# The last sixteenth of the first half of the output weights by six GpSimd transfers instead of SyncE's load

## The chip, the core and the metric

The kernel runs on one core of a Trainium2 chip. The metric is the device time of one execution in microseconds (us), the median of several runs. A profile of one execution gives the span from its first to its last instruction and the times of the single instructions and transfers in it; such times below count from the start of that span.

A core has five engines that run their own instruction streams beside each other: PE (TensorE, matmuls), DVE (VectorE), ACT (ScalarE), POOL (GpSimd) and SP (SyncE, which here only issues transfers and waits). They wait for each other through semaphores. Loads from HBM into the on-chip memory SBUF (128 partitions) are carried by 16 DMA engines.

## What is computed

One token is decoded: attention with 32 query heads over 4 cached key and value heads of 65,536 positions, a small gated MLP, and a gate that mixes the two. In short:

```python
def _A_ref(x, k_cache, v_cache, wq, wo):          # Hq 32, Hkv 4, Sk 65536, Dh 128, D 1024
    q = (x @ wq)...                               # 32 heads of 128
    scores = einsum('bhqd,bhkd->bhqk', q, k) * Dh ** -0.5
    o = einsum('bhqk,bhkd->bhqd', softmax(scores), v)
    return o.reshape(B, Sq, Hq * Dh) @ wo         # wo: 4096 x 1024

def _B_ref(x, w_in, w_sp, b_sp, w_out):           # F 3584, one position
    z = gelu(x @ w_in)
    z1, z2 = z[..., :F // 2], layernorm(z[..., F // 2:])
    return (z1 * (z2 * w_sp + b_sp)) @ w_out

g = sigmoid((x * gate_w).sum(-1))
out = g * _A_ref(...) + (1 - g) * _B_ref(...)
```

All inputs are bf16. The caches are 128 MB, the weights `wq` and `wo` 8 MB each.

## The kernel before

**The stream of loads.** Nearly everything that the kernel reads passes once through a ring in SBUF, `RING`, with five places of 16,384 bf16 columns (32 KB in each partition). The list `stream` holds the loads in the order in which they are wanted: `wq`, then keys and the MLP's weights, then pairs of key blocks (`load_k2`) and value blocks (`load_v2`), in the end the values 12 to 15 and the output weights `wo`. `load` appends to that list; `issue` turns entries into transfers on SP's queue, each as soon as the places it will overwrite have been given up (`done`), and always in the order of the list. A load waits for semaphores, on SP, until the last readers of each 1,024-column piece of its place (`("slot", i)`) have finished.

**The output weights** come last, in five loads. `("wo", 0, 0)` is the first half of the matrix, its rows 0 to 2047: partition p holds the sixteen rows 16p to 16p+15 side by side, 32 KB in all (the function `rows`, with c = 16). It goes to the first place of the ring, whose sixteen pieces hold key block 15 before. Then follow `("wo", 2, 0)` (2 MB) and the last quarter in pieces of 5, 2 and 1 eighths (`WO_CUT`: 1,280, 512 and 256 KB).

**The work at the end**, in the order in which it is queued on PE: `pv_piece(12)` to `(15)` multiply the probabilities with the values; `out_first(3)` sums the last group's denominators (L560); `wo_rows` multiplies the attention output of the first two groups with the first half of `wo`, sixteen rows per partition in a loop over c = 0..15, two halves of 512 columns each, into the PSUM tile `scp`; `out_rest(3)` scales and rearranges the last group's output (DVE, and PE at L582); `spin` runs a few matmuls whose results nobody reads; `spread` copies `scp` to SBUF on ACT (L661) and adds it to the final accumulator `fbt` with 16 matmuls (L665); `wo_piece(2)` and three `wo_piece(3, ...)` do the other half of `wo` (L717, 64 matmuls a quarter); a DVE cast (L778) and SP's store (L365) end it.

**How dependences are made.** `Recorder.op` takes an engine, a function, the keys that it reads and those that it writes, and works out the semaphore waits: an operation waits for the last writer of what it reads, and for the last writer and the readers of what it overwrites. A transfer's semaphore rises by 16 when it has landed. Every matmul pair shares its weights through `mm` (L258 to L264): the first of two loads them, which shows as L261, the second (L263) doesn't.

POOL's own work in this kernel is 36 small instructions: constants in the first 8 us, and four copies for each group of queries (`q_piece`, L487), the last at 244 us.

Of the kernel before, what the change touches and what calls it, by code (L numbers as in the profile page):

```python
# [138 lines left out]
def bass_gated_mix__gqa_block_cached__mixer_gmlp__decode_kernel(  # L139
# [19 lines left out]
    DO = A_wo.shape[1]  # L159
# [25 lines left out]
    OFF = {}  # L185
# [17 lines left out]
    arena = nc.alloc_sbuf_tensor("arena", [128, NA], BF16)  # L203
# [7 lines left out]
    def vw(base, off, dims, p0=0, np_=128):  # L211
        ps = base.ap[0][0]
        return bass.AP(tensor=base.tensor, offset=base.offset + off + p0 * ps,
                       ap=[[ps, np_]] + [list(d) for d in dims])
# [37 lines left out]
    KSC = lambda n: ("scp", n % 2)  # L252
# [3 lines left out]
    P = R.op  # L256

    def mm(e, loaded, *a, **kw):  # L258

        if not loaded:  # L260
            return e.matmul(*a, **kw)  # L261
        with nc.discard():
            one = e.matmul(*a, **kw).ins  # L263
        return e.add_instruction(dataclasses.replace(one, name=nc.get_next_instruction_name(), ldweights=False))  # L264
# [37 lines left out]
    stream = []  # L302
# [4 lines left out]
    def load(keys, src, off):  # L307

        n = len(stream)
        w = src.shape[1]  # L310
        for i, key in enumerate(keys):
            place[key] = (n, off + i * (w // len(keys)), w // len(keys))
        stream.append((keys, off, src))

    def rows(w, i, c):

        return w[128 * c * i:128 * c * (i + 1), :].rearrange("(p c) n -> p (c n)", c=c)
# [37 lines left out]
    WO_AT = [0, 8 * DO, 16 * DO, 24 * DO]  # L355
    WO_CUT = [(0, 5), (5, 7), (7, 8)]
    load([("wo", 0, 0)], rows(A_wo, 0, 16), WO_AT[0])
    load([("wo", 2, 0)], rows(A_wo, 2, 8), WO_AT[2])
    for c0, c1 in WO_CUT:
        load([("wo", 3, c0)], rows(A_wo, 3, 8)[:, DO * c0:DO * c1], WO_AT[3] + DO * c0)  # L360
# [11 lines left out]
    def grains(off, w):  # L372
        return list(range(off // GRAN, (off + w + GRAN - 1) // GRAN))

    def issue():

        while issued[0] < len(stream):
            n = issued[0]
            keys, off, src = stream[n]
            w = src.shape[1]  # L380
            gr = grains(off, w)
            if any(k not in used for x in gr if x in owner for k in owner[x]):
                return
            for j, x in enumerate(gr):
                owner[x] = (keys[j * len(keys) // len(gr)],)
            P("SP", lambda e, o=OFF["RING"] + off, w=w, src=src: e.dma_start(arena[:, o:o + w], src),
              w=[("slot", x) for x in gr], dma="s%d" % gr[0])
            issued[0] += 1

    def use(key):  # L390
        n, off, w = place[key]
        assert n < issued[0], key
        return arena[:, OFF["RING"] + off:OFF["RING"] + off + w], [("slot", x) for x in grains(off, w)]

    def done(key):
        used.add(key)
        issue()

    issue()


# [8 lines left out]
      r=["m32"], w=["sel"])  # L410
    P("DVE", lambda e: e.tensor_reduce(mq, vw(idf, 0, [[1, 16], [16, 8]]), AXX, ALU.add), r=["idf"], w=["mq"])
    P("DVE", lambda e: e.tensor_reduce(mhalf, vw(idf, 0, [[32, 2], [64, 2], [1, 32]]), mybir.AxisListType.XY, ALU.add),
      r=["idf"], w=["mhalf"])
# [4 lines left out]
    for fe in range(4):  # L418
        P("POOL", lambda e, fe=fe: e.tensor_copy(vw(sele, 128 * fe, [[32, 4], [1, 32]]),
                                                vw(idb, 64 * (fe // 2) + fe % 2, [[0, 4], [2, 32]])),  # L420
          r=["idb"], w=[KSE])
# [5 lines left out]
    def f(e):  # L427
# [7 lines left out]
      r=["oneb", "wsp", "bsp"], w=["mb"])  # L435
# [6 lines left out]
      r=["ones", "gs"], w=[KTB])  # L442
# [4 lines left out]
      r=["g"], w=["omg"])  # L447
# [3 lines left out]
    wqs, keys = use(("wq", 0))  # L451
# [242 lines left out]
    def wo_rows():  # L694
        sl, keys = use(("wo", 0, 0))

        def f(e):
            for c in range(16):
                j = c % 4
                z = 31 + 32 * c  # L700
                for s in range(2):
                    o = DO * c + 512 * s
                    ins = mm(e, s > 0, scp[32 * j:32 * j + 1, 512 * s:512 * (s + 1)], ovz[:, z:z + 1], sl[:, o:o + 512],
                             start=(c < 4), stop=(c >= 12), tile_position=(0, 32 * j),
                             skip_group_check=True)
            return ins
        P("PE", f, r=[("ovec", 0), ("ovec", 1)] + keys, w=[KSC(0)])
        done(("wo", 0, 0))

    def wo_piece(i, c0=0, c1=8):  # L710
# [54 lines left out]
    for n in (12, 13, 14, 15):  # L765
        pv_piece(n)
        if n < 14:
            pt_half(n + 2)
    out_first(3)
    wo_rows()  # L770
    out_rest(3)
    spin(2)
# [39 lines left out]
```

## Time and profile before

| | |
|---|---|
| median of 3 runs | 380.71 us (380.64 to 380.71) |
| span of the profiled execution | 379.59 us |
| read from HBM | 162.01 MB, 427 GB/s over the span |
| busy PE / DVE / ACT / POOL | 229.6 / 204.7 / 23.3 / 8.2 us |
| share of DMA in the chain that ended last | 68% |
| value load 12 (v12) landed | 338.80 us |
| value load 14 (v14) landed | 358.11 us |
| first half of `wo` issued, landed | 329.4, 367.75 us |
| next quarter of `wo` landed | 372.61 us |
| last quarter's three pieces landed | 375.72, 376.95, 377.55 us |

The profiled execution's span and the median of the runs differ by 1.12 us; that lies outside the first and last instruction. A landing is the time of a transfer's last semaphore increment: the loads raise theirs by one for each of the 16 DMA engines, so the trace has sixteen times for each load. It also has a record of every packet that a DMA engine moved, with its queue, size, start and duration, but not with the number of the engine. Engines' busy times overlap and do not add up to the span; what matters is which wait ends last at each place.

### The profile page before, as it was taken

The page shows a single profiled execution, that of the slowest core. Times are in us where ns is not written, and L with a number is a line of the kernel's source. Part 1 is how long each engine was busy: PE and PEld are TensorE (multiplying, and loading weights), DVE is VectorE, ACT ScalarE, POOL GpSimd, SP SyncE. Part 2 cuts the span into 40 slices and gives each one's busy share as a digit, 9 for nine tenths or more (in the row PEclk, how much of TensorE's full clock was granted, in tenths as well). Part 3 has the DMA queues.
Part 4 walks back from the last instruction along what each step waited for, and adds up shares of the span by engine and source line. Part 5 has one row for each costly group of instructions (what it writes and reads, how often), then busy time and mean ns, then how long its engine had stood idle before and what let it go on. Part 6 is the DMA issues. An engine that isn't in the chain of part 4 may idle for free.

```text
span 379.6 us, 2565 instructions
## 1 busy us (share of the span) xinstructions
PE 229.6 (60%) x1444; PEld 57.4 (15%) x835; DVE 204.7 (54%) x162; ACT 23.3 (6%) x24; POOL 8.2 (2%) x36
## 2 busy tenths in 40 slices
PE   0061488458558923895389428952896199737296
PEld 0010011011111200122012001220111011211024
DVE  4011496778389524974597248745773387412021
ACT  1000000010420000002200000022000000220000
POOL 5000000000000000000000000000000000000000
PEclk9997599696859985998599859995799589958599
DMA  9999999999999999999999999999999999999996
GB/s 442 421 414 394 483 388 439 439 453 391 437 442 442 442 430 435 435 442 442 442 430 394 421 442 442 444 435 428 435 435 437 435 442 442 430 421 414 418 428 263
DMA packets 3662, 162.17 MB, mean 427 GB/s; under 512 B 452, under 2 KB 452, under 8 KB 708
## 3 DMA queue, kind: packets, MB, share of 16 engines
q1 hardware_dynamic: 3616, 162.01, 98.9%
q8 instruction: 9, 0.15, 0.1%
q10 hardware_dynamic: 36, 0.00, 0.0%
q14 instruction: 1, 0.01, 0.0%
HBM read 162.01 MB, written 0.00 MB: 427 GB/s over the span
## 4 chain that ended last, share of the span: by engine, by line
DMA 68%; PE 16%; DVE 14%; ACT 1%; issue 1%; ACTq 0%; SPq 0%
DMA arena<-in_A_k_cache_dram 47%; DVE arena L499 12%; DMA arena<-in_A_wo_dram 8%; DMA arena<-in_A_v_cache_dram 7%; PE scp L261 6%; PE scp L263 5%; DMA arena<-in_B_b_sp_dram 5%; PE obt L261 2%; PE obt L263 2%; DVE arena L536 1%; PE fbt L717 1%; ACT arena L531 1%; ACTq L288 0%; PE fbt L665 0%; ACT arena L661 0%
## 5 line engine op out<-in xcount | busy, mean ns | idle before, releaser
L499 DVE STREAM_TRANSPOSE arena<-arena 128x2048 f32<-128x2048 f32 x64 | 143.0, 2284 | 56.7 <-DMA arena<-in_A_k_cache_dram 41.8
L261 PE MATMUL scp<-arena 128*128 128x512 bf16 (+1 forms) x274 | 111.5, 423 | 95.7 <-DVE arena L499 95.4
L263 PE MATMUL scp<-arena 128*128 128x512 bf16 (+1 forms) x275 | 110.4, 418 | 0.0
L261 PE MATMUL obt<-arena 128*64 128x512 bf16 (+2 forms) x334 | 61.4, 410 | 14.2 <-DMA arena<-in_A_v_cache_dram 14.2
L263 PE MATMUL obt<-arena 128*64 128x512 bf16 (+2 forms) x334 | 61.0, 408 | 0.0
L261 PEld LDWEIGHTS scp<-arena 128*128 128x128 bf16 (+1 forms) x274 | 27.4, 104 | 206.6 <-issue 103.5
L536 DVE STREAM_TRANSPOSE arena<-arena 128x2048 bf16<-128x2048 bf16 x7 | 16.2, 2311 | 27.0 <-PE obt L263 24.8
L531 ACT ACTIVATE arena<-arena 128x2048 bf16<-128x2048 f32 x8 | 16.0, 2002 | 218.4 <-DVE arena L528 195.0
L261 PEld LDWEIGHTS obt<-arena 128*64 128x64 bf16 (+1 forms) x334 | 17.9, 111 | 65.7 <-issue 59.0
L516 DVE TENSOR_SCALAR_CACHE_REDUCE arena<-scp 128x2048 f32<-128x2048 f32 x8 | 18.3, 2291 | 16.0 <-PE scp L263 16.0
L565 DVE RECIPROCAL arena<-mbt 128x1 f32<-128x1 f32 x4 | 0.6, 139 | 17.5 <-PE mbt L560 17.5
L539 DVE STREAM_TRANSPOSE arena<-arena 128x1024 bf16<-128x1024 bf16 x2 | 2.5, 1245 | 12.9 <-PE obt L263 12.9
L487 POOL COPY arena<-arena 32x32 bf16<-32x32 bf16 x16 | 3.2, 203 | 234.4 <-PE scp L263 209.8
L434 PE MATMUL mbt<-arena 1*128 1x2 bf16 x1 | 0.2, 159 | 12.2 <-DMA arena<-in_B_b_sp_dram 12.2
L436 DVE COPY arena<-mbt 128x2 f32<-128x2 f32 x1 | 0.2, 159 | 12.2 <-PE mbt L434 12.2
L578 PE MATMUL mbt<-arena 128*64 128x128 bf16 x8 | 1.3, 313 | 7.7 <-DVE arena L572 7.7
L429 PE MATMUL scp<-arena 8*128 8x1 bf16 x8 | 0.7, 198 | 8.6 <-DVE arena L424 8.6
L717 PE MATMUL fbt<-arena 128*32 128x128 bf16 x128 | 4.1, 220 | 1.2 <-DMA arena<-in_A_wo_dram 1.2
L778 DVE CAST arena<-fbt 36x128 bf16<-36x128 f32 x1 | 0.3, 282 | 7.2 <-PE fbt L717 7.2
L528 DVE TENSOR_REDUCE arena<-mbt 128x1 f32<-128x32 f32 x4 | 0.8, 192 | 6.0 <-PE mbt L525 6.0
L717 PEld LDWEIGHTS fbt<-arena 128*32 128x32 bf16 x128 | 3.6, 97 | 2.4 <-issue 1.2
L464 DVE CAST arena<-obt 97x1024 bf16<-97x1024 f32 x1 | 1.2, 1225 | 4.8 <-PE obt L263 4.8
(92 smaller groups left out, 54.9 us busy)
## 6 DMA issues: line engine op xcount, KB each, us to landing
arena<-in_A_k_cache_dram SPq DMA_DIRECT2D x2, 4096.0 KB, 33.3
arena<-in_B_w_in_dram SPq DMA_DIRECT2D x1, 7168.0 KB, 30.5
arena<-in_A_wo_dram SPq DMA_DIRECT2D x1, 4096.0 KB, 38.3
arena<-in_B_w_out_dram SPq DMA_DIRECT2D x1, 3584.0 KB, 21.4
arena<-in_A_wo_dram SPq DMA_DIRECT2D x1, 2048.0 KB, 27.2
arena<-in_A_wo_dram SPq DMA_DIRECT2D x1, 1280.0 KB, 29.9
arena<-in_A_wo_dram SPq DMA_DIRECT2D x1, 512.0 KB, 30.7
arena<-in_A_wo_dram SPq DMA_DIRECT2D x1, 256.0 KB, 30.8
```

The lines of the kernel that those rows point to most:

```text
L261: return e.matmul(*a, **kw)
L263: one = e.matmul(*a, **kw).ins
L464: P("DVE", lambda e: e.tensor_copy(psb[0:97, :], ob[0:97, :]), w=["psb", "ob"])
L487: P("POOL", lambda e, pb=pb: e.tensor_copy(vw(qpad, 24 + 32 * pb, [[QP, 4], [1, 8]], 32 * pb, 32), vw(qall, 8 * g, [[32, 4], [1, 8]], 32 * ...
L499: P("DVE", lambda e: e.transpose(ktb(i).bitcast(F32), sl[:, 4096 * p:4096 * (p + 1)].bitcast(F32)), r=keys[4 * p:4 * p + 4], w=[("kt", i % ...
L516: P("DVE", lambda e: e.tensor_scalar(scs(j), scp[:, :], 0.0, None, op0=ALU.add, op1=ALU.max, accum_out=maxc[:, j:j + 1]), w=[("sc", j % 2) ...
L528: P("DVE", lambda e: e.tensor_reduce(gcol(g, K_NB), mb[:, 0:32], AXX, ALU.min), w=[("nb", g), "mb"])
L531: P("ACT", lambda e: e.activation(psb2, scs(j), ACTF.Exp, bias=gcol(j // 2, K_NB), scale=SCALE, accum_out=lp[:, j:j + 1]), r=[("sc", j % 2 ...
L536: P("DVE", lambda e: e.transpose(ptsb2, psb2), r=["psb"], w=[("ptsb", 0), ("ptsb", 1)])
L539: P("DVE", lambda e: e.transpose(ptsb(n), ab("PSB", 1024, 1024 * (n % 2))), r=["psb"], w=[("ptsb", n % 2)])
L578: ins = e.matmul(mb[64 * g:64 * (g + 1), 0:128], vw(sel, 128 * c, [[2, 64]]), osc[:, 128 * c:128 * (c + 1)], start=(c == 0), stop=(c == 3) ...
L717: ins = e.matmul(fb[32 * b:32 * (b + 1), 0:QW], ovz[:, z:z + 32], sl[:, o:o + QW], start=False, stop=(i == 3 and c == 7), tile_position=(0 ...
```

## The change

SP's load of the first half of `wo` is cut by one sixteenth: it brings 15 of each partition's 16 rows. The sixteenth row of each (c = 15; 2 KB in a partition, 256 KB in all) is loaded by POOL in six transfers that take 16, 51, 4, 34, 6 and 17 partitions, one after the other on POOL's queue. The first waits for the readers of the sixteenth piece of the ring's place; the others wait for nothing of their own and follow it. Each row is fetched as two pieces of 512 columns, in swapped order, so that the first 512 columns of the place hold the second half of the row; `wo_rows` reads them accordingly for c = 15. All six raise one semaphore, and `wo_rows` waits for them too. Each is issued with `single_packet=True`.

```diff
     load([("wo", 0, 0)], rows(A_wo, 0, 16), WO_AT[0])
+    SPLIT = (len(stream) - 1, 15)
+    SHARES = (16, 51, 4, 34, 6, 17)
+    assert sum(SHARES) == 128
     load([("wo", 2, 0)], rows(A_wo, 2, 8), WO_AT[2])
...
                 owner[x] = (keys[j * len(keys) // len(gr)],)
+            if n == SPLIT[0]:
+                w = DO * SPLIT[1]
+                spread_rows(OFF["RING"] + off + w, src[:, w:], ("slot", gr[SPLIT[1]]))
+                src, gr = src[:, :w], gr[:SPLIT[1]]
             P("SP", lambda e, o=OFF["RING"] + off, w=w, src=src: e.dma_start(arena[:, o:o + w], src),
               w=[("slot", x) for x in gr], dma="s%d" % gr[0])
             issued[0] += 1
+
+    def spread_rows(o, src, key):
+
+        p0 = 0
+        for i, n in enumerate(SHARES):
+            dst = vw(arena[:, o:o + 1], 0, [[512, 2], [1, 512]], p0, n)
+            s0 = src[p0:p0 + n, :]
+            s0 = bass.AP(tensor=s0.tensor, offset=s0.offset + 512, ap=[list(s0.ap[0]), [-512, 2], [1, 512]])
+            P("POOL", lambda e, dst=dst, s0=s0: e.dma_start(dst, s0, single_packet=True),
+              w=[key] if i == 0 else [("share", i)], dma="sw")
+            p0 += n
...
-                    o = DO * c + 512 * s
+                    o = DO * c + 512 * (s if c < SPLIT[1] else 1 - s)
...
-        P("PE", f, r=[("ovec", 0), ("ovec", 1)] + keys, w=[KSC(0)])
+        P("PE", f, r=[("ovec", 0), ("ovec", 1)] + keys + [("share", i) for i in range(1, len(SHARES))], w=[KSC(0)])
```

## The prediction

> **What bounds the kernel now.** I read the page first. Its slices say that the loads never pause, and its queue table that they are all SyncE's (q1):
>
> ```profile
> DMA  9999999999999999999999999999999999999996
> ...
> q1 hardware_dynamic: 3616, 162.01, 98.9%
> q8 instruction: 9, 0.15, 0.1%
> q10 hardware_dynamic: 36, 0.00, 0.0%
> ```
>
> The 16 DMA engines are busy from start to end, so time is bytes over rate, but for the last slice. The chain of waits in order of time, over the end, shows what comes then (start, us, what):
>
> ```profile
> 345.79 29.93 DMA arena<-in_A_wo_dram
> 375.72 0.14 issue
> 375.86 2.16 PE fbt L717 x64
> 378.01 0.02 issue
> 378.04 0.28 DVE arena L778
> ```
>
> The chain gives the whole 2.16 us to PE. The timeline adds that PE's last eight weight loads wait once more:
>
> ```profile
> 377.59 0.23 PEld L717 LDWEIGHTS fbt<-arena 128*32 128x32 bf16 x8 [0.15 <-DMA arena<-in_A_wo_dram]
> ```
>
> That is the last load, of 256 KB; 2.0 us of fixed work follow its landing (eight weight loads and matmuls, the cast, the store). So the end is set by the last engine to deliver its sixteenth of that load. The table of stretches shows how evenly the engines get there (after the stretch: its length, busy PE, PEld, DVE, ACT, POOL; the last two columns are the DMA share and GB/s):
>
> ```profile
> 375.20:375.50 0.30, 0.17 (x1) 0.00 (x0) 0.00 (x0) 0.00 (x0) 0.00 (x0) 1.00 1.04 416
> 375.50:375.90 0.40, 0.04 (x2) 0.07 (x4) 0.00 (x0) 0.00 (x0) 0.00 (x0) 1.00 0.65 261
> 375.90:376.20 0.30, 0.30 (x13) 0.30 (x15) 0.00 (x0) 0.00 (x0) 0.00 (x0) 1.00 0.59 239
> ...
> 376.40:376.70 0.30, 0.30 (x19) 0.30 (x14) 0.00 (x0) 0.00 (x0) 0.00 (x0) 1.00 0.57 219
> ...
> 376.90:377.10 0.20, 0.20 (x14) 0.19 (x10) 0.00 (x0) 0.00 (x0) 0.00 (x0) 1.00 0.22 82
> ```
>
> The share falls to about 10/16 at 375.5 and stays there for over a microsecond: six engines are out of work, ten are not. The sixteen increments of the last load's semaphore say it engine by engine: six at 375.87 to 375.95, one at 376.21, nine from 376.76 to 377.55. The cause is in the packet records: nine times before, an instruction fetch (q8, 16 KB, eight times; q14, 8 KB, once) took an engine out of its stream. The one at 329.57 lasted 0.94 us, where a 16 KB packet of q1 takes 0.61, and the 64 KB packet behind it took 2.92 us for 2.42: 1.4 us lost. Every load is cut into sixteen equal parts, so an engine once late stays late. Idle share times length from 375.5 on sums to 0.9 us; that is all that perfect levelling could give.
>
> **The change, part by part.**
>
> *Removed from SP's load.* Each of 128 rows goes from 32 KB to 30 KB. Packets of 32 KB take 1.213 us and of 16 KB 0.611, so 2 KB is 0.075; with eight rows on each engine, each sheds 0.60 us.
>
> *Added on the POOL queue.* Each row comes as two pieces of 1 KB. Packets of 2 KB take 84 ns, of 256 B 18 ns, of 4 B 9 ns; on that line 1 KB is 46 ns (38 if the fixed part is paid once for many). Six completions at 9 ns add 0.05 on each engine, if each posts on all sixteen.
>
> *Who carries them.* No trace row shows a POOL transfer. Those of 128 rows go to all engines evenly, and ACT's two loads of 8 rows are 16 packets of 256 B: one row to an engine. I take it that a transfer goes to the largest number of engines up to 16 that divides its rows: 16 rows to 16 engines, 51 to three by 17, 4 to four, 34 to two by 17, 6 to six, 17 to one. The last five fill 3+4+2+6+1 = 16 engines once if each starts where the one before stopped. So six engines get 18 rows, ten get 2: as many as the trace has early and late ones. That they are the same ones the trace can't show, as packets carry no engine number; the equal counts are why I lean to it. [...]
>
> *Sum by engine.* Light: 4 x 0.046 + 0.05 - 0.60 = **-0.36** (-0.40 at 38 ns). Heavy: 36 x 0.046 + 0.05 - 0.60 = **+1.12** (+0.81). The last landing, on a light engine, goes from 377.55 to 377.19; the heavy ones go from 375.95 to 377.07, just below.
>
> *Cost of a visit.* A POOL packet sits between two of SP's. ACT's small ones cost their own 9 to 18 ns, and the 64 KB packets behind them kept their 2.418: lower bound, nothing more. Upper bound: a fetch lost 1.4 us for data worth 0.61, 0.8 over; six visits would be 4.8. I take the lower, since ACT's, like POOL's, are data and completions for SBUF, and a fetch is not.
>
> *When they come.* POOL waits only for slot 15's reader, the last k transpose (L499), which ends at 319.56, and POOL has no other work left. SP issues the shortened load behind v14 as now, at 329.43. So the six travel inside v12's stream and push v12 and v14 back by 0.24 on the late engines (338.80 and 358.11 become 339.04 and 358.35). That moves pv_piece(12) to (15), hence out_first(3) and out_rest(3), by 0.24. wo_rows now starts at 367.80, just behind the load's landing at 367.75 (367.39 after); it would start at 368.04 behind PE's queue, be done at 369.9, and spread's matmuls would end at 372.1 instead of 371.9. The next load lands at 372.61 - 0.36 = 372.25: 0.1 of cover left. Were it gone, wo_piece(2) would slip, which spin(3) and the wait to 375.36 hide (0.5 now). SP's issue of wo 3 waits for pv_piece(12) (345.42, then 345.66) with the ring full to 372: free. GpSimd's own time for six issues is unknown, but has 48 us until wo_rows. PE's wait for the six is one more instruction.
>
> *Total.* -0.36 on the last landing; the 2.0 us behind it are the same. Span 379.59 to 379.23; with the 1.12 between span and median (380.71), **380.35 us**.
>
> **The rivals.**
>
> *No levelling* (the six are dealt out evenly, or the equal split was no loss). Each engine gets 8 rows back: 16 x 0.046 + 0.05 - 0.60 = +0.19, **380.9**. Against it: 51, 34 and 17 do not split evenly. [...]
>
> *The shares sit on the wrong engines*: the slower case that I weigh most. If the engine that is latest now carries 18 rows, it lands at 377.55 + 1.12 = 378.67: **381.83**. It decides as soon as one heavy engine is late by over 0.25 us (377.19 - 1.12 = 376.07, against 375.95 or less for the six). For it: no number of an engine in the trace, and an unknown start of the dealing. [...]
>
> *A fetch meets a heavy engine.* The trace has a tenth fetch, at 377.16, in PE's matmuls for the second-last load; it meets an engine that is already idle. With everything 0.36 earlier it comes at 376.80. If it goes to an engine not yet hit, that is one of the six, and their packets now end 376.63 to 376.78 (375.51 to 375.66 plus 1.12). On an overlap of a packet or two the engine loses up to 1.4: 377.07 + 1.42 = 378.49, **381.65**. The margin is 0.02; cheaper pieces (38 ns) widen it to 0.33.
>
> *The six land late.* ACT's one-element loads landed at 16.54 and 21.37 because each packet waited a turn of 2.42 behind SP's. If each 1 KB piece took its own turn, a heavy engine needs 42 turns, and from 319.6 SP's ring has 32 packets until 372. wo_rows would wait till about 375 instead of 367.8, with spread (1.0 + 1.1), wo_piece(2) (2.0), spin (0.8) and the last 64 matmuls (2.1) behind it: some 6 us, **386.7**. Against it: the code asks for a single packet. [...]
>
> **How the numbers follow.** Levelling as summed 0.52; no levelling 0.08; wrong engines 0.15; the fetch 0.12; late landing or dear visits 0.07; 0.06 for a gain that I have no mechanism for (a light engine cannot shed over 0.60, so it would have to come from other fetches moving). A measurement of this kernel tells about 0.2%, 0.76 us, from no change. The first two lie within it: same 0.60. The next three are slower: 0.34. Faster 0.06. The likeliest case alone spans 380.25 (-0.45, all 12 KB at full rate and visits free) to 380.7. The range, 380.2 to 381.9, adds the wrong engines and the fetch.
>
> **What would show it.** Right: a POOL queue with 262,144 bytes and landings by 350; packets that fill the stretch 375.5 to 376.6 (share near 1 where it is 0.6); the last load's sixteen increments within 0.4 us of each other, the last near 377.2; wo_rows waiting for PE's queue, not for a load. Wrong: increments still spread over 1.5 us or more (engines), a fetch between the last packets (fetch), wo_rows later than 368.5 (late landing), or SP's packets longer than 2.42 behind each POOL packet (visits).

## The result, and the profile after

The changed kernel takes **388.71 us** (median of 4 runs, 388.55 to 389.93) where the kernel before takes 380.71 beside it (380.64 to 380.94): a ratio of 1.0217 [1.0203, 1.0232], **slower by 8.0 us**. The forecast was 380.35. The profiled execution is the longest of the four: 389.93 us, with a span of 388.5, which is 8.9 more than before. Times below compare this span with the one before.

The slices and the queue table of the page after:

```profile
span 388.5 us, 2572 instructions
...
DMA  9999899999999999999999999999999999999991
...
DMA packets 4238, 162.17 MB, mean 417 GB/s; under 512 B 948, under 2 KB 948, under 8 KB 1284
...
q1 hardware_dynamic: 3616, 161.75, 97.3%
q0 software_dynamic: 576, 0.27, 0.3%
```

The queue q0 is POOL's and has moved what it should. But it did so in 576 packets, and the last slice, which was at 6 tenths, is at 1: the stream of loads no longer reaches to the end. The chain of waits over the end (start, us, what) shows what does:

```profile
371.05 0.54 PE mbt L578 x4
371.58 4.98 another core or an unknown queue
376.56 0.14 issue
376.70 0.60 PE scp L261 x4
...
380.35 1.03 ACT arena L679
...
381.42 1.07 PE fbt L683 x16
382.49 1.79 PE fbt L735 x64
...
385.03 1.92 PE fbt L735 x64
386.95 0.02 issue
386.97 0.28 DVE arena L796
```

The chain doesn't know the releaser of the second line; it ends at 376.56, when the semaphore of the six transfers is full. The timeline of the same kernel names the wait on PE's side, in the brackets:

```profile
319.25 4.84 POOL L404 DMA_DIRECT2D arena<-in_A_wo_dram  x6 [73.95 <-DVE arena L517]
...
376.70 0.60 PE L261 MATMUL scp<-arena 128*1 128x512 bf16 x4 [5.12 <-DMA arena<-in_A_wo_dram]
```

So `wo_rows` (scp) started at 376.70, before at 367.80: 8.9 us later, as much as the spans differ by. Behind it stands work that the loads used to cover: `spread` on ACT (L679) and PE (L683), `wo_piece(2)` and the last `wo_piece` (L735). The six were issued at 319.25 and took 57 us to land. The last piece of SP's stream came at 381.04 (before 377.55) and PE was not waiting for it: its 64 weight loads at L735 ran through in one group, without the second wait of before.

The stream itself also got slower. The table of stretches, after (stretch, length, busy time of PE, PEld, DVE, ACT, POOL, then PEclk, DMA share, GB/s):

```profile
319.20:329.20 10.00, 9.74 (x78) 2.94 (x41) 3.37 (x5) 2.10 (x2) 4.84 (x6) 1.00 1.03 423
329.20:339.00 9.80, 0.61 (x4) 0.34 (x4) 4.09 (x7) 2.09 (x2) 0.00 (x0) 0.67 0.99 403
339.00:350.00 11.00, 8.39 (x64) 2.04 (x32) 2.49 (x2) 0.00 (x0) 0.00 (x0) 0.83 1.06 415
350.00:360.00 10.00, 0.00 (x0) 0.00 (x0) 0.00 (x0) 0.00 (x0) 0.00 (x0) 0.65 0.88 354
360.00:370.00 10.00, 8.68 (x56) 2.45 (x30) 0.00 (x0) 0.00 (x0) 0.00 (x0) 0.67 0.98 394
...
376.70:381.00 4.30, 4.30 (x38) 0.83 (x21) 0.29 (x1) 0.65 (x1) 0.00 (x0) 0.58 0.74 301
```

The same stretches before:

```profile
329.20:339.00 9.80, 1.12 (x10) 0.74 (x9) 4.71 (x7) 2.10 (x2) 0.00 (x0) 0.60 1.00 430
339.00:350.00 11.00, 9.84 (x64) 2.19 (x30) 2.36 (x2) 0.00 (x0) 0.00 (x0) 0.74 1.00 435
350.00:360.00 10.00, 1.75 (x10) 0.58 (x6) 0.13 (x1) 0.00 (x0) 0.00 (x0) 0.58 1.00 433
360.00:370.00 10.00, 9.80 (x99) 3.02 (x51) 1.90 (x4) 0.24 (x1) 0.00 (x0) 0.91 0.94 406
```

From 329.2 to 370 the rate is lower by 27, 20, 79 and 12 GB/s; times the lengths that is 1.4 MB less, or 3.2 us at 433 GB/s. The first half of `wo` on SP's queue indeed landed 3.2 us later (370.93 for 367.75). Over half of that, 1.8 us, comes from 350 to 360 alone, where the run with the wait hidden, below, with the same six transfers, has 392 GB/s and not 354. While `wo_rows` ran, from 376.70 to 380.35, the granted clock was 0.50, and it took 3.6 us; before, it had 1.00 and took 1.9.

**How POOL's packets went.** q0's records are 32 packets of 2 KB and 48 of 4 KB with data, 64 of 8 B and 336 of 16 B without, and 96 of 4 B (the semaphore: six transfers times sixteen engines). The data are dealt as the prediction had it: the first transfer 2 KB to each of 16 engines, the 51 rows to three engines (eight packets of 4 KB and one of 2 KB each), 4 rows to four, 34 to two, 6 to six, 17 to one. But an engine that has no rows of a transfer gets as many small packets instead: all sixteen make the fullest engine's 1+9+1+9+1+9 data turns and six completions, 36 in all (576 packets over sixteen engines). From 323.38 to 376.12 each of these turns waited for one packet of SP's, and SP's packets get shorter towards the end: on average an engine moved 14.4 of 64 KB (2.60 us each), 8 of 30 KB (1.21), 8 of 16 KB (0.66), 2.3 of 10 KB (0.41) and 4 completions (0.01) in that time, 36.7 packets of SP's and 53 us in all. Two things add up: many turns, and at each a packet of SP's to wait for. The experiments take them apart.

### The profile page after: what moved, and what is told of

Read it like the earlier page. It is cut to its first block, busy times and chain, and to the rows that moved or that the text cites. A ratio compares the mean times of both kernels' runs of the same rounds, so it can differ in the third digit from the quotient of the medians.

```text
span 388.5 us, 2572 instructions
## 1 busy us (share of the span) xinstructions
PE 230.2 (59%) x1444; PEld 57.5 (15%) x835; DVE 204.5 (53%) x162; ACT 23.3 (6%) x24; POOL 13.1 (3%) x42
## 4 chain that ended last, share of the span: by engine, by line
DMA 60%; PE 21%; DVE 16%; another core or an unknown queue 1%; ACT 1%; issue 1%; ACTq 0%; SPq 0%
DMA arena<-in_A_k_cache_dram 46%; DVE arena L517 15%; DMA arena<-in_A_v_cache_dram 8%; PE scp L261 6%; PE scp L263 6%; DMA arena<-in_B_b_sp_dram 5%; PE obt L261 3%; PE obt L263 3%; PE fbt L735 1%; DVE arena L554 1%; PE fbt L683 1%; ACT arena L549 1%; ACT arena L679 1%; ACTq L288 0%
## 5 line engine op out<-in xcount | busy, mean ns | idle before, releaser
L404 POOL DMA_DIRECT2D arena<-in_A_wo_dram x6 | 4.8, 810 | 74.0 <-DVE arena L517 74.0
L609 DVE TENSOR_TENSOR arena<-mbt,arena 64x128 f32<-64x128 f32 (+1 forms) x4 | 1.2, 290 | 9.0 <-PE mbt L600 7.8
L735 PE MATMUL fbt<-arena 128*32 128x128 bf16 x128 | 3.9, 219 | 0.0
```

Source lines behind the costliest of these rows:

```text
L404: P("POOL", lambda e, dst=dst, s0=s0: e.dma_start(dst, s0, single_packet=True), w=[key] if i == 0 else [("share", i)], dma="sw")
L735: ins = e.matmul(fb[32 * b:32 * (b + 1), 0:QW], ovz[:, z:z + 32], sl[:, o:o + QW], start=False, stop=(i == 3 and c == 7), tile_position=(0 ...
```

## The experiments

"Full" is the time at which POOL's semaphore was full; "mean landing" is the mean of the last load's sixteen increments (before: 376.68, the last at 377.55), which tells what the stream lost without the spread among engines.

**One transfer of 128 rows.**

```diff
-    SHARES = (16, 51, 4, 34, 6, 17)
+    SHARES = (128,)
```

> The same 256 KB by POOL, but as one transfer of 128 rows instead of six. Turn theory (every packet of POOL's ring waits behind one packet of SP's on the same DMA engine, and all sixteen engines make the 36 turns of the six transfers, with stuffing where they have no rows): 8 rows of two pieces are 4 packets of 4 KB and a completion on each engine, 5 turns instead of 36; the semaphore is full by 323.4 + 5 x 2.7 = 337, far ahead of the load's landing near 368, and wo_rows waits for the load again; 381 to 382 us (0.19 for the dearer pieces, and up to 1 if SP's loads run 8% slower for those 12 us). Rival, POOL's transfers are late as such (GpSimd writes descriptors slowly, or the pieces of 1 KB are slow): 256 KB are 256 KB, wo_rows waits again to about 376 and it stays near 388. Rival, the unequal shares load six engines too much: fixed here, 381 as well; e2_short tells it from the first.

380.89 us (380.60 to 381.06), ratio 1.0004 [0.9995, 1.0013]. Full at 337.86, mean landing 376.49, SP's 64 KB packets 2.421 us. Five turns on each engine:

```profile
q0 software_dynamic: 80, 0.26, 0.2%
```

The same bytes by the same queue cost nothing when they come in 80 packets and not 576. What is slow is how they are dealt, and not that GpSimd carries them.

**Shorter turns.** SP's two value loads ahead of the half are cut to packets of 16 KB; as a control, the same in the kernel before.

```diff
-            P("SP", lambda e, o=OFF["RING"] + off, w=w, src=src: e.dma_start(arena[:, o:o + w], src),
+            m = 16384 if SPLIT[0] - 2 <= n < SPLIT[0] else 65536
+            P("SP", lambda e, o=OFF["RING"] + off, w=w, src=src, m=m: e.dma_start(arena[:, o:o + w], src, max_dma_last_dim=m),
```

> The six transfers as they are; only SP's loads of the values 12 and 14 come in pieces of 16 KB instead of 64 KB, so that a turn behind one of SP's packets lasts 0.66 us instead of 2.4 to 2.7. Turn theory: 36 turns x 0.66 are 24 us, the six are in by 347 to 350, wo_rows waits for the load again, and the time is 380.7 plus what the visits cost the stream: 381 to 383. Rival, lateness of POOL's transfers as such, or six overloaded engines: neither is changed by SP's piece size, the semaphore fills near 376 again and it stays near 388.5. If the visits cost SP's stream a fixed amount each (0.1 us), its last landing stays 3.5 us late; if the stream runs 8% slower only while POOL's ring holds work, it is 1.5 to 2 us late.

> The kernel before with the values 12 and 14 in pieces of 16 KB: the control for e2_short. Each piece pays some 9 ns more than its bytes (a packet of 16 KB takes 0.611 us, one of 64 KB 2.418): 48 more packets on each engine are 48 x 9 = 0.43 us. 381.1, by every theory.

The control: 381.00 (380.79 to 381.19), ratio 1.0007 [0.9997, 1.0016]; short packets alone cost little. The changed kernel with them: **383.14** (382.90 to 383.47), 1.0065 [1.0050, 1.0080]. POOL still has 576 packets, but is full at 350.01. Its chain of waits ends on SP's last load again:

```profile
347.19 30.37 DMA arena<-in_A_wo_dram
377.56 0.14 issue
377.70 1.77 PE fbt L736 x56
379.47 0.04 issue
379.51 0.42 PE fbt L736 x8
```

So the wait is the number of turns times the length of a packet of SP: POOL's packets now pass in 25 us (324.26 to 349.57), 0.70 a turn behind packets of 0.63 to 0.68 us, where the changed kernel's 64 KB packets took 2.60. The wait goes, and 5.6 of the 8.0 us with it. 2.4 us stay, and the mean landing (378.78) has 2.1 of them; the short packets themselves account for 0.3, by the control.

**The wait hidden.** The sixteenth row leaves `wo_rows` and is multiplied by eight small matmuls behind `wo_piece(2)`, straight into `fbt`.

```diff
-            for c in range(16):
+            for c in range(15):
...
+    def wo_last():
+        sl, keys = use(("wo", 0, 0))
...
+            for s, b, j in SLOTS:
+                o = DO * 15 + (QW * s + 512) % DO
+                z = 31 + 32 * 15 - j
+                ins = e.matmul(fb[32 * b:32 * (b + 1), 0:QW], ovz[:, z:z + 32],
+                               sl[:, o:o + QW], start=False, stop=False,
...
+    wo_last()
```

> The six transfers and SP's load as in the changed kernel; the row c = 15 is taken out of wo_rows and multiplied behind wo_piece(2) by eight matmuls straight into the final accumulator, so nothing but those eight waits for the six. Turn theory: the six still land near 376.5, but wo_rows starts with the load near 371, and the end is again the last landing of the last load, 381.0 in the changed kernel, plus 2.0: span 383.1, 384.2 us. That leaves +3.5 of the +8.0 as the price that SP's stream pays for the visits, and 4.5 as the wait of wo_rows with its slow clock. Rival, the whole loss is one thing, the late semaphore: 380.4 to 381.

**383.45** (383.38 to 383.51), 1.0072 [1.0057, 1.0087], although POOL is full only at 375.96. The chain of waits ends on the load:

```profile
346.44 31.79 DMA arena<-in_A_wo_dram
378.23 0.14 issue
378.36 2.13 PE fbt L748 x64
```

With the transfers as they were and only their reader moved, 5.3 of the 8.0 us go: this is the price of `wo_rows` waiting, its slow clock included. The other 2.7 are the price on SP's stream (mean landing 379.38, 2.7 later). Two experiments that change different things agree on this division within 0.3 us, or 0.6 when the 0.3 of the short packets is taken off the first.

**Without `single_packet`.**

```diff
-            P("POOL", lambda e, dst=dst, s0=s0: e.dma_start(dst, s0, single_packet=True),
+            P("POOL", lambda e, dst=dst, s0=s0: e.dma_start(dst, s0),
```

> The changed kernel without single_packet=True. The trace of the changed kernel shows POOL's data in packets of at most 4 KB (four pieces of 1 KB) with the flag set. If the flag does nothing there: 576 packets on POOL's queue, 36 turns, the six full near 376, 388 to 390 us. If it does something, packets and turns get more and it is slower than 389.

388.47 (388.13 and 388.81), 1.0205 [1.0185, 1.0226]; packets of the same number and sizes, full at 375.21. In the queue table:

```profile
q0 software_dynamic: 576, 0.27, 0.3%
```

The flag did nothing in this kernel. A packet held at most four pieces of 1 KB with it and without it. The mean landing is 378.96 here, 2.3 later than before.

**Is it the small packets?** My first theory for the stream's 2.7 us was the packets without data. Eight equal transfers have none; (96, 15, 17) has them, with the same 16 turns.

```diff
-    SHARES = (16, 51, 4, 34, 6, 17)
+    SHARES = (16,) * 8
```

> The same rows by POOL in eight transfers of 16 rows, one row to each engine in each: no engine is without rows, so there is no stuffing; 8 x (1 packet of 2 KB and 1 completion) = 16 turns, in by 323.4 + 16 x 2.43 = 362, before the load. Stuffing theory (SP's packets slow down behind the stuffing packets of 4 to 16 bytes and not behind data): SP's 64 KB packets keep their 2.42 us, last landing within 0.5 of the kernel before, 380.5 to 381.2. Rival, every visit and every additional transfer costs SP's stream 0.1 us: 16 visits, last landing +1.6, 382 to 382.5.

> The same rows by POOL in three transfers of 96, 15 and 17 rows: also 16 turns (4 + 2 + 10), but of these nine are stuffing of 16 bytes on fifteen engines, while the one with the 17 rows has data; one engine carries 24 rows. Stuffing theory: SP's 64 KB packets take 2.5 to 2.7 us while the 17 rows are under way, the mean landing of the last load is 1 to 1.5 us later than in e5_nostuff, 382 to 383 us. Rival, visits cost the same whatever they carry: the mean landing as in e5_nostuff, and the time differs from it by the loaded engine alone (16 more rows, 1.3 us on one engine). The mean over the engines, not the last one, tells the two apart.

The theory fell. Eight equal transfers, 256 packets of which none is of 16 or 8 B: 383.94 (383.31 to 384.96), 1.009 [1.007, 1.011], mean landing 379.49, full at 361.77. With stuffing, (96, 15, 17): 382.49 (382.07 to 382.89), 1.0048 [1.0033, 1.0063], mean landing 377.83, full at 360.19. The one without is the dearer one. SP's 64 KB packets took 2.70 us on average in 324 to 334 there. In the other kernel they took 2.60 while the 96 rows were under way (323.7 to 334.9), and these have no stuffing; from 340.1 on, while the 17 rows and their stuffing were, 2.46.

**The shares on SP's queue.** Whole rows of 2 KB, on the queue that carries the rest, in shares of 64, 51 and 13.

```diff
-    SHARES = (16, 51, 4, 34, 6, 17)
+    SHARES = (64, 51, 13)
...
-            P("POOL", lambda e, dst=dst, s0=s0: e.dma_start(dst, s0, single_packet=True),
+            P("SP", lambda e, dst=dst, s0=s0: e.dma_start(dst, s0),
```

> The row c = 15 on SP's own queue, in whole rows of 2 KB, by transfers of 64, 51 and 13 rows: no POOL, no turns, no stuffing. If SP's transfers are dealt by the largest divisor too, three engines get 4 + 17 + 1 = 22 rows, ten get 5 and three get 4. Tests what levelling alone would bring: if the three are early ones, the late engines shed 3 to 4 rows, 0.25 to 0.3 us, the last landing goes from 377.55 to 377.3, and 380.4 us. If one of the three is late: 14 rows more, 1.1 us, 381.8. The six landing late has no part in it by any theory.

381.86 (381.51 to 381.97), 1.0029 [1.0017, 1.0041]. There are no turns between queues here, and it is still 1.2 us slower. The expectation had 381.8 for a late engine that carries 14 rows more, but that is not what happened: the mean landing is 377.70, 1.0 later, and the last only 0.8 behind that, so that it wasn't the loaded engines alone that were late. While three engines moved the 51 rows, SP's first 30 KB packets rose to as much as 1.94 us (undisturbed they take 1.138), and the 2 KB packets took 0.09 to 0.24 for 0.084. So rows that come in such shares disturb the other packets on SP's queue too.

**Are several transfers under way the trouble?** Four transfers of 32 rows, and the same with each waiting for the one before.

```diff
-    SHARES = (16, 51, 4, 34, 6, 17)
+    SHARES = (32,) * 4
...
-              w=[key] if i == 0 else [("share", i)], dma="sw")
+              w=[key, ("share", 0)] if i == 0 else [("share", i), ("share", i - 1)], dma="sw")
```

> The stuffing theory has fallen: without stuffing, eight transfers slowed SP's packets as much. What is left goes with the number of POOL's transfers that are under way together: one alone (e1_even) left SP's 64 KB packets at 2.42 us, three cost the mean landing of the last load 1.1 us, eight 2.8. Here the rows come by four transfers of 32 (one packet of 4 KB and one completion on each engine in each: 8 turns), issued one right after the other. Theory of transfers under way together: SP's packets take 2.55 to 2.8 us for the 20 us that the turns last, mean landing 0.8 to 1.4 late, 381.4 to 382.2 us. Rival, only the number of turns counts: e1_even's 5 turns cost nothing, so 8 cost next to nothing, 380.7 to 381.0.

> As e8_four, but each transfer is issued only when the one before has landed, so that one at a time is under way; the same 8 turns, packets and bytes. Theory of transfers under way together: SP's packets stay at 2.42 us, 380.6 to 381.1, though the last of the four lands later (four times some 7 us, near 350, still before the load). Rival, turns or transfers as such: as e8_four.

Together: 382.54 (382.25 to 390.22 in seven runs), 1.0060 [1.0031, 1.0090]. One at a time: 382.51 (382.18 to 385.63 in six), 1.0069 [1.0039, 1.0099]. No difference, so this theory fell too. The traces are of executions of 386.54 and 384.85 us, longer than the medians. In the second's, 64 KB packets were slow while a transfer had its visits (means of 2.45 to 2.9 in steps of 2 us) and back at 2.42 to 2.46 between the transfers.

**Neighbouring rows, or rows apart?** The same four and eight transfers, but transfer i takes partitions i, i + 4, i + 8 and so on (i + 8 for eight): each is spread over all 128 partitions.

```diff
-    SHARES = (16, 51, 4, 34, 6, 17)
+    SHARES = (32,) * 4
...
-            dst = vw(arena[:, o:o + 1], 0, [[512, 2], [1, 512]], p0, n)
-            s0 = src[p0:p0 + n, :]
+            dst = vw(arena[:, o:o + 1], 0, [[512, 2], [1, 512]], i, n)
+            dst = bass.AP(tensor=dst.tensor, offset=dst.offset, ap=[[len(SHARES) * dst.ap[0][0], n], [512, 2], [1, 512]])
+            s0 = src[i:i + 1, :]
...
-            s0 = bass.AP(tensor=s0.tensor, offset=s0.offset + 512, ap=[list(s0.ap[0]), [-512, 2], [1, 512]])
+            s0 = bass.AP(tensor=s0.tensor, offset=s0.offset + 512, ap=[[len(SHARES) * s0.ap[0][0], n], [-512, 2], [1, 512]])
```

> e9_serial was as slow as e8_four, so the number of transfers under way together is not the reason either. What e1_even has and the others lack: each of its engines moves rows that lie 8 partitions (and 256 KB of wo) from its neighbour's; in the others the sixteen engines work on the same 16 to 51 neighbouring partitions at a time. Here four transfers of 32 rows as in e8_four, but transfer i takes the partitions i, i+4, i+8, ..., all over SBUF. Crowding theory: SP's 64 KB packets keep 2.42 us, mean landing of the last load within 0.3 of the kernel before, 380.6 to 381.1. Rival, more than one transfer as such: as e8_four, 382.3 or more.

> As e5_nostuff, eight transfers of 16 rows, but transfer i takes the partitions i, i+8, i+16, ...: the same 16 turns, packets and bytes as there, one row for each engine in its own eighth partition. Crowding theory: 380.6 to 381.2, SP's packets at 2.42. Rival, more than one transfer as such: as e5_nostuff, 383.3 to 385.

Four apart: **380.79** (380.59 to 380.89), 1.0002 [0.9993, 1.0012], mean landing 376.56, SP's 64 KB packets 2.418 to 2.421, 128 packets on q0 as with four neighbouring ones. Eight apart: 381.51 (381.27 to 381.99), 1.0019 [1.0010, 1.0029], above the 380.6 to 381.2 that was expected; mean landing 377.11, SP's 64 KB packets 2.44 to 2.48, 256 packets as with eight neighbouring ones. The first stretch in which POOL's packets run beside SP's, with eight transfers of neighbouring rows:

```profile
324.00:334.00 10.00, 6.16 (x54) 2.25 (x30) 4.45 (x7) 2.10 (x2) 0.13 (x1) 0.86 0.99 382
```

and with eight transfers of rows apart:

```profile
324.00:334.00 10.00, 5.69 (x48) 2.08 (x26) 4.69 (x8) 2.10 (x2) 0.00 (x0) 0.94 1.00 428
```

382 against 428 GB/s (421 in the same stretch before), with the same bytes, packets and turns. Which rows a transfer takes changes the price on the stream: 1.8 us to nothing for four transfers (382.54 to 380.79), 3.2 to 0.8 for eight (383.94 to 381.51).

Why it does is not shown, and being neighbours can't be all of it. The 96 rows of (96, 15, 17) cover three quarters of the partitions, six rows to an engine, and while they were under way, ahead of the other two transfers, SP's 64 KB packets took 2.60 us. With all 128 rows in one transfer they took 2.42. The stretch 324 to 334 with the 96 rows, and with the 128:

```profile
324.00:334.00 10.00, 5.64 (x50) 2.05 (x28) 4.74 (x8) 2.10 (x2) 0.00 (x0) 0.99 0.99 394
324.00:334.00 10.00, 6.16 (x56) 2.12 (x31) 4.81 (x9) 2.10 (x2) 0.00 (x0) 0.91 1.04 446
```

The rate of a stretch also depends on where packets of 64 KB begin and end (446 with the 128 rows and 421 before, at the same 2.42 us a packet), so the packets' length is the surer measure.

No trace shows which rows an engine takes; the expectation for four apart assumed that they are dealt in order. On that assumption another reading, a conjecture too, fits as well: an engine's packets are slow when its POOL rows are not among the eight that SP's loads give it. With eight apart 0.8 us stays by either. No run separates the two.

## Why the prediction was wrong

**The step that failed is *When they come*.** It let the six "travel inside v12's stream" and land by 350. They landed at 376.56, behind 36 turns. The step had the issue right (319.25, forecast 319.56), and the rival *the six land late* had the mechanism and nearly the count (42 turns; 36 measured), but was given 0.07 on one argument, the flag, which the run without it showed to do nothing (576 packets and 0.27 MB either way). The 36 pieces of a heavy engine did share packets: POOL's data came in 48 of 4,096 B, four pieces each, and 32 of 2 KB, none larger, which makes ten for 18 rows. What the rival did not have is that all sixteen engines make the fullest one's turns.

**The rival's price was too small as well**: 386.7 for 388.71. It had `wo_rows` at about 375; in the profiled execution it was 376.70 (1.7 more). It took `wo_rows` at the 1.9 us of before; after 5.1 us of idle PE it ran at a granted clock of 0.50 and took 3.6 (1.7 more). With the wait hidden PE had not been idle before it, and the clock was 1.00. The profiled execution of the changed kernel took 389.93, 3.2 more than the rival's 386.7, and the two terms make 3.4. In the run without the flag (388.81 in the profiled execution, 2.1 more) they are 0.3 and 1.7.

***Cost of a visit*: the lower bound was the wrong end.** The step took 9 to 18 ns and had SP's packets keep 2.418 us. The mean landing is 3.66 us later over 36 turns in the profiled execution, the longest of the four; it is 2.70 later with the wait hidden and 2.28 without the flag, with the same packets. That is 0.06 to 0.1 a turn on average, between the bounds (0.8 above). But it isn't a price of each visit: four transfers with rows apart make eight turns and cost nothing. The six of this change take neighbouring rows, as the dear ones do.

**Right in the working**: *Who carries them*, the rows' dealing by divisors, as the packets show (48 of 4 KB and 32 of 2 KB). That the six engines with 18 rows (eight packets of 4 KB each) are early ones follows from joining each packet to the one that ended just before it, as far as such joins are unambiguous: when the six were issued, seven engines started 64 KB packets at 318.0 to 318.8 and nine at 319.3 to 319.9. The seven are the late ones: their next packets come at 320.4 to 321.2, some 1.1 to 1.6 us behind the nine's, and seven instruction fetches had met the stream by then. The six are among the nine, at 319.32 to 319.71. A seventh of the nine, at 319.45, lost its lead to the fetch at 329.6. *Removed from SP's load* was right by its packets: 30 KB take 1.138 us undisturbed, 0.075 less than 32 KB. That one transfer of 128 rows took 380.89, where the rival *no levelling* had 380.9, can't bear it out, since the run isn't told from no change; POOL's four packets and completion there are worth 0.66 on each engine (0.163 and 0.009 each) for the 0.60 removed.

**The gain that was forecast, -0.36, is too small to show in the times.** Last less mean landing was 0.87 before, and 0.77 with one transfer of 128 rows and in the control. It is 0.69 in the changed kernel, 0.68 with short turns, 0.66 with the wait hidden, 0.47 without the flag: levelling took some 0.1 to 0.4 us off, on engines that the disturbance had just made uneven, beside 2.1 to 3.7 us lost on the mean. The increments were forecast within 0.4 us of each other and span 1.8 (379.25 to 381.04).

So of the 8.0 us, 5.3 are the wait of `wo_rows`, shown by moving its reader, and 2.7 the stream's loss, levelling included. That the turns make the wait is shown; why these rows slow the stream stays open. No version here beats the kernel before; one with few turns, uneven shares and rows apart wasn't tried, and by the spread it could win 0.9 us at most.

## What to carry to other kernels

Before a transfer goes to a second queue beside long packets, count its turns on the fullest engine (pieces, packets, completions of every transfer) and add up the other queue's packets that they will wait for: 36 turns took 53 us here and ended after the reader wanted the data, 5 took 13. One transfer over all partitions cost nothing here. Where it must be several, try rows spread evenly over all of them: four transfers of every fourth row cost nothing, four of 32 consecutive ones 1.8 us. And price a late operand with the granted clock of the work that waited: here 0.50 for 1.00, 3.6 us for 1.9.

## What the runs showed of the hardware

- A POOL transfer over fewer than sixteen engines gave the others packets of 16 or 8 B, as many as the fullest got data (by their counts and sizes): 400 of 576 packets moved no data and posted no semaphore.
- POOL's data packets were never above 4 KB, with `single_packet` or without (48 of 4,096 B and 32 of 2 KB with it; the same numbers and sizes without).
- Transfers over neighbouring rows slowed the packets of SP's queue (64 KB: 2.42 to 2.70 us on average over 10 us with eight transfers); every fourth row did not (2.42), every eighth did a little (2.44 to 2.48). One transfer of 96 rows did too (2.60), one of 128 did not (2.42). The runs changed the places in SBUF and the rows in HBM together, so which of the two the price goes with stays open.
- In the profiled execution of four neighbouring transfers (386.54 us) SP's packets stayed long after POOL's last one (343.70) to the end: 2.71 us for 64 KB, 1.274 for 30 KB. With one transfer at a time (384.85 us) the 30 KB packets after POOL's last one (358.8) took 1.274. The runs don't explain that.
